# A gated product written without gaps, an fp32 tanh for GpSimd and a later turn for ScalarE's output copies, in an RG-LRU and gated linear unit kernel

## The chip, the cores and the metric

The kernel runs on one core of a Trainium2 chip. Five engines work at the same time, each through its own instructions in order: TensorE (PE in the profile, with its weight loads as PEld), VectorE (DVE), ScalarE (ACT), GpSimd (POOL) and SyncE (SP), which here only issues DMA transfers. The metric is the device time of one execution in microseconds (us); lower is better.

## The reference

Inputs are x, r_gate and i_gate, each 4 x 6336 x 256 in fp32, a vector a_param of 256, and three weights. The first half is a gated linear recurrence over time, the second half a gated linear unit with a causal convolution of 5 taps on its gate.

```python
log_a = 8.0 * sigmoid(r_gate) * log(clip(sigmoid(a_param), 1e-6, 1 - 1e-6))
a_t = exp(log_a)
x_gated = sqrt(maximum(1 - a_t * a_t, 1e-6)) * sigmoid(i_gate) * x
for t in range(S):
    h = a_t[:, t] * h + x_gated[:, t];  y[:, t] = h
gate_pre = sum(conv_w[k] * shifted(y, 4 - k) for k in range(5))
out = (sigmoid(gate_pre) * (y @ w_val)) @ w_out
```

## The kernel before

**Windows.** The 4 x 6336 = 25344 tokens are cut into 50 windows of 512 tokens (the last has 256). In a window, partition p holds the 4 tokens 4p to 4p+3 (index j), so that a load or a store is 4 KB without gaps for each partition.

**The operations of a window**, in the order in which they depend on each other, with their engines and lines:

- `load` (SP, L164): three transfers of 512 KB, r and i into the tile `ri`, x into `xt`, three buffers each.
- `tanh` (ACT, L238): one instruction over both gates, 2048 elements for each partition, fp32 in, bf16 out, into `tri`. Sigmoids are built as (1 + tanh(z/2)) / 2.
- `u2` (POOL): L245 adds 1 to the i half of `tri`, bf16 in, fp32 out, into the single buffer `t1` (named t in the profile); L246 multiplies that by x, bf16 out, into the ring `uring`.
- `srT` (PE, L226): 8 transposes bring the r half to channels on partitions. `exp` (ACT, L261) makes a_t from it, two instructions of 512 elements, into the ring `aring`; it reads the transposed tile with a step, so that tokens come out in their order in time.
- `e` (POOL, L267): a_t squared, fp32, into `ering`. `sq` (ACT, L276 or L282): the square root 0.5 sqrt(1 - e), written as bf16 over `ering`. Sqrt stands in another function table than Tanh and Exp, so each change costs a table load on ACT. The roots of several windows are done together, as a unit.
- `uT` (PE, L226): 8 transposes of `uring`. `scan` (DVE): for each of the two channel halves, L299 multiplies uT (PSUM, read with a step) by the root into `xg`, and L304 scans the recurrence in time, into the ring `yring` in bf16.
- `conv` (PE, L331): 10 matmuls with diagonal weights into `gp`. `tg` (ACT, L338): tanh of the gate. `val` (PE, L347): y times w_val, 4 matmuls into PSUM.
- `gv` (DVE, L356): (tg + 1) times val into `gv`, the left operand of the last product. tg and val have tokens in order of time, t = 4p + j; gv has the layout [j, h, p], so that the 128 tokens with the same j stand side by side.
- `out` (PE, L368): for each half of a window (index q), 4 matmuls with w_out into the PSUM tile `ops`. `osb` copies it to SBUF, on DVE (L379) or on ACT (L381). `store` (SP, L385).

**What sets the order.** `make_plan` (L29 to L116) is a list scheduler that runs when the program is built. It holds a cost for each operation (COST, L20), simulates the five engines, and always takes the candidate with the smallest start time, then the smallest priority number (`min(cands)`, L104). The instructions are then written out in the order of these planned start times, so each engine's queue is fixed. A cost changes no instruction, only the order. The dependencies that the plan sees, with buffer counts, are the lists of pairs: ("u2", -NTRI) means that u2 of three windows before must be done. Both engines are offered for `osb` at L86 and L87, with priority 0.5 for each; on ACT, `tg` has 0, `exp` 1, `tanh` 3 and `sq` -1.

**Units of square roots.** A unit starts when DVE has little left to scan (`low`, L97) and enough windows are ready: at least MIN_UNIT (L19), 1, 2, 3 and 4 for the first four units, 4 for each later one, or when the rings of NS = 11 windows are full (`stuck`).

**Buffers in PSUM.** srT, uT, xg, gp, val and ops have one buffer each, so a writer on PE waits for the reader on DVE or ACT of the window (or the half) before.

Of the kernel before, what the change touches and what calls it, by code (L numbers as in the profile page):

```python
# [8 lines left out]
P = 128  # L9
WIN = 512  # L10
SUB = WIN // P
CONV_K = 5
C_SCALE = 8.0
NS = 11
NY = 7
NIN = 3
NTRI = 3
NOSB = 3
MIN_UNIT = [1, 2, 3, 4]  # L19
COST = dict(load=3.9, tanh=1.9, u2=3.3, srT=0.5, uT=0.5, exp=1.45, e=2.15, scan=3.75, conv=2.45, tg=1.0,  # L20
            val=0.95, gv=1.2, out=0.5, osbD=0.68, osbA=0.6, sq=0.88, sq0=0.2, table=1.3, store=1.3,
            sem=0.15, dma=2.2)
FP32 = mybir.dt.float32
BF16 = mybir.dt.bfloat16
ACT = mybir.ActivationFunctionType
ALU = mybir.AluOpType


def make_plan(frac):  # L29

    nw = len(frac)
    nq = [max(1, round(2 * f)) for f in frac]
    qwin = [(g, i) for g in range(nw) for i in range(nq[g])]
    qlast = [sum(nq[:g + 1]) - 1 for g in range(nw)]
    done, nxt, free = {}, {}, {}
    order, units = [], []
    mode = "E"  # L40

    def at(op):
        return nxt.get(op, 0)

    while True:
        cands = []

        def cand(op, eng, dur, deps, prio, i, n=1):
            t = 0.0
            for d in deps:  # L50
                if d[1] < 0:
                    continue
                if d not in done:
                    return
                t = max(t, done[d] + COST["sem"])
            if eng == "ACT" and op != "osb" and (op == "sq") != (mode == "S"):
                dur = dur + COST["table"]
            cands.append((max(free.get(eng, 0.0), t), prio, op, eng, dur, i, n))

        def per_window(op, eng, prio, deps, limit=nw):  # L60
            g = at(op)
            if g < limit:
                cand(op, eng, COST[op] * frac[g], [(d, g + o) for d, o in deps], prio, g)

        nsq = at("sq")
        per_window("load", "DMA", 0, [("tanh", -NIN), ("u2", -NIN)])
        per_window("tanh", "ACT", 3, [("load", 0), ("srT", -NTRI), ("u2", -NTRI)])
        per_window("u2", "POOL", 1, [("tanh", 0), ("uT", -NS)])
        per_window("srT", "PE", 0, [("tanh", 0), ("exp", -1)])
        per_window("exp", "ACT", 1, [("srT", 0), ("scan", -NS), ("e", -NS)])  # L70
        per_window("e", "POOL", 0, [("exp", 0), ("scan", -NS)])
        per_window("uT", "PE", 1, [("u2", 0), ("scan", -1)], nsq)
        per_window("scan", "DVE", 2, [("uT", 0), ("sq", 0), ("val", -NY), ("conv", 1 - NY)], nsq)
        per_window("conv", "PE", 3, [("scan", 0), ("tg", -1)])
        per_window("tg", "ACT", 0, [("conv", 0), ("gv", -2)])
        per_window("val", "PE", 2, [("conv", 0), ("gv", -1)])
        g = at("gv")
        if g < nw:
            cand("gv", "DVE", COST["gv"] * frac[g],
                 [("tg", g), ("val", g), ("out", qlast[g - 2] if g >= 2 else -1)], 1, g)  # L80
        q = at("out")
        if q < len(qwin):
            cand("out", "PE", COST["out"], [("gv", qwin[q][0]), ("osb", q - 1)], 1, q)
        q = at("osb")
        if q < len(qwin):
            for e, eng in (("D", "DVE"), ("A", "ACT")):  # L86
                cand("osb", eng, COST["osb" + e], [("out", q), ("store", qwin[q][0] - NOSB)], 0.5, q)  # L87
        g = at("store")
        if g < nw:
            cand("store", "DMA", COST["store"] * frac[g], [("osb", qlast[g])], -1, g)  # L90

        n = at("e") - nsq
        if n and mode == "E":
            all_in = at("exp") == nw
            stuck = at("e") == at("exp") and (all_in or ("scan", at("exp") - NS) not in done
                                              and at("exp") >= NS)
            low = (nsq - at("scan")) * (COST["scan"]) <= 2 * COST["table"] + COST["sq"] * n  # L97
            enough = n >= min(MIN_UNIT[min(len(units), len(MIN_UNIT) - 1)], nw - nsq)
            if stuck or (low and enough):
                cand("sq", "ACT", COST["sq0"] + COST["sq"] * sum(frac[nsq:nsq + n]),  # L100
                     [("e", nsq + n - 1)], -1, nsq, n)
        if not cands:
            break
        t, prio, op, eng, dur, i, n = min(cands)  # L104
        free[eng] = t + dur
        order.append((t, op, i, eng, n))
        nxt[op] = i + n
        for k in range(i, i + n):
            done[(op, k)] = t + dur + (COST["dma"] if eng == "DMA" else 0.0)
        if op == "sq":  # L110
            units.append(n)
        if eng == "ACT" and op != "osb":
            mode = "S" if op == "sq" else "E"
    assert at("store") == nw
    order.sort(key=lambda o: o[0])
    return order, qwin  # L116
# [3 lines left out]
def kernel(  # L120
# [11 lines left out]
    nc = tc.nc  # L132
    B, S, D = x.shape
# [10 lines left out]
    ntok = [min(WIN, T - g * WIN) for g in range(nwin)]  # L144

    segs = []
    for g in range(nwin):
        t0, t1 = g * WIN, g * WIN + ntok[g]
# [3 lines left out]
    plan, qwin = make_plan([n / WIN for n in ntok])  # L152

    const = ctx.enter_context(tc.tile_pool(name="const", bufs=1))
    inp = ctx.enter_context(tc.tile_pool(name="inp", bufs=3))
    live = {}
# [10 lines left out]
    with tc.manual_schedule():  # L167
# [19 lines left out]
        with tc.tile_pool(name="ps_setup", bufs=1, space=bass.MemoryType.PSUM) as ps_setup:  # L187
# [6 lines left out]
                                    op0=ALU.mult, op1=ALU.add)  # L194
            nc.vector.tensor_scalar(out=ksig[:], in0=ksig[:], scalar1=1e-6, scalar2=1.0 - 1e-6,
                                    op0=ALU.max, op1=ALU.min)
# [9 lines left out]
        for h in range(H):  # L206
            for kk in range(CONV_K):
                nc.vector.tensor_scalar(out=diag[:, h, kk, :], in0=ident_f[:], scalar1=wcol[:, h, kk:kk + 1],
                                        scalar2=None, op0=ALU.mult)
# [4 lines left out]
        work = ctx.enter_context(tc.tile_pool(name="work", bufs=2))  # L214
# [5 lines left out]
        uring = rings.tile([P, NS, SUB, D], BF16, name="uring")  # L220
        yring = rings.tile([P, H, NY * WIN], BF16, name="yring")

        def transposes(dst, src, g):
            for h in range(H):
                for j in range(ntok[g] // P):
                    nc.tensor.transpose(out=dst[:, h, j * P:(j + 1) * P],  # L226
                                        in_=src[:, j, h * P:(h + 1) * P],
                                        identity=ident_b[:])
# [5 lines left out]
        def op_tanh(g, eng, n):  # L234
            nj = ntok[g] // P
            ri = live.pop(("ri", g))
            tri = inp.tile([P, 2, SUB, D], BF16, name="tri", tag="tri", bufs=NTRI)
            nc.scalar.activation(out=tri[:, :, 0:nj, :], in_=ri[:, :, 0:nj, :], func=ACT.Tanh, scale=0.5)  # L238
            live["tri", g] = tri

        def op_u2(g, eng, n):
            nj = ntok[g] // P
            xt, tri = live.pop(("xt", g)), live["tri", g]
            t1 = work.tile([P, SUB, D], FP32, name="t1", tag="t1", bufs=1)
            nc.gpsimd.tensor_scalar(out=t1[:, 0:nj, :], in0=tri[:, 1, 0:nj, :], scalar1=1.0, scalar2=None, op0=ALU.add)  # L245
            nc.gpsimd.tensor_tensor(out=uring[:, g % NS, 0:nj, :], in0=t1[:, 0:nj, :], in1=xt[:, 0:nj, :],  # L246
                                    op=ALU.mult)

        def op_srT(g, eng, n):
            srT = psum.tile([P, H, WIN], BF16, name="srT", tag="srT", bufs=1)  # L250
            transposes(srT, live["tri", g][:, 0], g)
            live["srT", g] = srT

        def by_token(t, h, g):
# [96 lines left out]
        def op_gv(g, eng, n):  # L351
            gv = work.tile([P, SUB, H, P], BF16, name="gv", tag="gv", bufs=2)
            tg, val = live.pop(("tg", g)), live.pop(("val", g))
            nj = ntok[g] // P
            for hs in ([slice(0, H)] if nj == SUB else [slice(h, h + 1) for h in range(H)]):
                nc.vector.scalar_tensor_tensor(  # L356
                    out=gv[:, 0:nj, hs, :].rearrange("c j h p -> c (h p) j"),
                    in0=tg[:, hs, 0:ntok[g]].rearrange("c h (p j) -> c (h p) j", j=nj), scalar=1.0,
                    in1=val[:, hs, 0:ntok[g]].rearrange("c h (p j) -> c (h p) j", j=nj), op0=ALU.add, op1=ALU.mult)
            live["gv", g] = gv  # L360

        def op_out(q, eng, n):
# [20 lines left out]
        def op_store(g, eng, n):  # L383
            nj = ntok[g] // P
            nc.sync.dma_start(of[g * WIN:g * WIN + nj * P, :].rearrange("(p j) d -> p j d", j=nj),  # L385
                              live.pop(("osb", g))[:, 0:nj, :])

        ops_by_name = dict(load=op_load, tanh=op_tanh, u2=op_u2, srT=op_srT, exp=op_exp, e=op_e, sq=op_sq,
                           uT=op_uT, scan=op_scan, conv=op_conv, tg=op_tg, val=op_val, gv=op_gv,
                           out=op_out, osb=op_osb, store=op_store)  # L390
        for (t, op, i, eng, n) in plan:
# [31 lines left out]
```

## Time and profile before

| | |
|---|---|
| runs | 521.2 and 520.99 us, median 521.1 |
| the profiled execution | 518.84 us, span 517.1 us |
| mean granted TensorE clock | 0.826 |
| instructions | 5526 |
| moved by DMA | 104.44 MB, mean 202 GB/s |

The span runs from the first to the last instruction of one profiled execution. A row of a group names the line, the engine, the operation, out<-in with partitions x elements and type, and the count; behind the first bar come busy time and the mean of one in ns, behind the second the idle time of the engine just before these instructions and what ended it. A row of a stage gives its limits, its length, and for each engine the busy time with the count of instructions; behind them the granted clock (1.00 is full speed), the busy share of the 16 DMA engines, and GB/s. A row of waits reads: who waited <- for whom: total us, times, longest. A row of the timeline has start, duration, engine, line, operation and, in brackets, the idle time before it with what ended it. A row of one line's durations has min/median/max in ns.

### The profile page before, as it was taken

The page shows a single profiled execution, that of the slowest core. Times are in us where ns is not written, and L with a number is a line of the kernel's source. Part 1 is how long each engine was busy: PE and PEld are TensorE (multiplying, and loading weights), DVE is VectorE, ACT ScalarE, POOL GpSimd, SP SyncE. Part 2 cuts the span into 40 slices and gives each one's busy share as a digit, 9 for nine tenths or more (in the row PEclk, how much of TensorE's full clock was granted, in tenths as well). Part 3 has the DMA queues.
Part 4 walks back from the last instruction along what each step waited for, and adds up shares of the span by engine and source line. Part 5 has one row for each costly group of instructions (what it writes and reads, how often), then busy time and mean ns, then how long its engine had stood idle before and what let it go on. Part 6 is the DMA issues. An engine that isn't in the chain of part 4 may idle for free.

```text
span 517.1 us, 5526 instructions
## 1 busy us (share of the span) xinstructions
PE 322.3 (62%) x1971; PEld 181.2 (35%) x1971; DVE 451.9 (87%) x320; ACT 325.3 (63%) x312; POOL 347.8 (67%) x158
## 2 busy tenths in 40 slices
PE   1342865667565576667767665775766766756563
PEld 0222433334333343434433333433433333423232
DVE  3243999978999979999989999999999979999993
ACT  6969667498665774847575685597476594365221
POOL 4999969969965965948773986957948859400000
PEclk9975779876987976989886888798887887899875
DMA  8975754869845467457755774575845651201112
GB/s 281 380 249 207 259 205 148 302 227 326 317 157 215 164 230 259 162 190 252 264 181 210 268 264 170 196 288 189 296 166 200 209 184 75 82 35 47 81 41 103
DMA packets 29386, 104.44 MB, mean 202 GB/s; under 512 B 3239, under 2 KB 3758, under 8 KB 29358
## 3 DMA queue, kind: packets, MB, share of 16 engines
q1 hardware_dynamic: 28814, 103.83, 55.9%
q0 software_dynamic: 544, 0.26, 0.4%
q8 instruction: 15, 0.25, 0.2%
q14 instruction: 13, 0.11, 0.1%
HBM read 78.39 MB, written 25.95 MB: 202 GB/s over the span
## 4 chain that ended last, share of the span: by engine, by line
DVE 45%; issue 31%; PE 12%; ACT 4%; DMA 4%; SPq 0%; DVEq 0%; ACTq 0%
DVE gv L356 19%; DVE yring L304 11%; DVE xg L299 10%; DVE osb L379 4%; PE ops L368 4%; DMA out_dram<-osb 3%; PE gp L331 3%; PE val L347 3%; ACT tri L238 2%; PE uT L226 1%; DMA ri<-in_i_gate_dram 1%; PE srT L226 1%; ACT aring L261 1%; ACT osb L381 0%; ACT ering L282 0%
## 5 line engine op out<-in xcount | busy, mean ns | idle before, releaser
L356 DVE SCALAR_TENSOR_TENSOR gv<-tg,val 128x1024 bf16<-128x1024 bf16 (+1 forms) x51 | 232.9, 4574 | 10.7 <-ACT tg L338 5.1
L267 POOL TENSOR_TENSOR ering<-aring 128x1024 f32<-128x1024 f32 (+1 forms) x50 | 93.8, 1878 | 94.3 <-ACT aring L261 90.0
L245 POOL TENSOR_SCALAR t<-tri 128x1024 f32<-128x1024 bf16 (+1 forms) x50 | 137.2, 2745 | 20.8 <-ACT tri L238 16.2
L331 PE MATMUL gp<-yring,diag 128*128 128x512 bf16 (+13 forms) x580 | 143.8, 402 | 4.3 <-DVE yring L304 4.2
L304 DVE TENSOR_TENSOR_SCAN yring<-aring,yring,xg 128x512 bf16<-128x512 f32 (+4 forms) x98 | 120.6, 1231 | 3.5
L368 PE MATMUL ops<-wo,gv 128*128 128x256 bf16 x396 | 76.1, 327 | 72.3 <-DVE gv L356 37.9
L246 POOL TENSOR_TENSOR uring<-t,xt 128x1024 bf16<-128x1024 f32 (+1 forms) x50 | 116.7, 2334 | 4.2
L381 ACT COPY osb<-ops 128x512 f32<-128x512 f32 x53 | 31.0, 585 | 126.4 <-PE ops L368 104.8
L347 PE MATMUL val<-yring,wv 128*128 128x512 bf16 (+1 forms) x200 | 65.1, 459 | 61.4 <-DVE gv L356 61.4
L238 ACT ACTIVATE tri<-ri 128x2048 bf16<-128x2048 f32 (+1 forms) x50 | 93.9, 1896 | 1.4 <-DMA ri<-in_i_gate_dram 1.4
L299 DVE TENSOR_TENSOR xg<-uT,ering 128x512 f32<-128x512 bf16 (+1 forms) x100 | 76.0, 760 | 20.1 <-ACT ering L282 15.0
L331 PEld LDWEIGHTS <-diag 128*128 128x128 bf16 x580 | 59.2, 112 | 74.4 <-issue 36.3
L338 ACT ACTIVATE tg<-gp 128x1024 bf16<-128x1024 f32 (+1 forms) x50 | 50.8, 1016 | 47.1 <-PE gp L331 46.9
L368 PEld LDWEIGHTS <-gv 128*128 128x128 bf16 x396 | 42.5, 113 | 98.5 <-DVE gv L356 57.5
L261 ACT ACTIVATE aring<-srT,khf 128x512 f32<-128x512 bf16 (+1 forms) x100 | 72.1, 776 | 6.8 <-PE srT L226 5.6
L226 PE MATMUL srT<-ident_b,tri 128*128 128x128 bf16 x396 | 35.5, 241 | 28.5 <-ACT tri L238 28.3
L347 PEld LDWEIGHTS <-wv 128*128 128x128 bf16 x200 | 21.7, 110 | 82.4 <-issue 72.7
L226 PE MATMUL uT<-ident_b,uring 128*128 128x128 bf16 x396 | 36.6, 246 | 21.6 <-DVE xg L299 21.6
L379 DVE COPY osb<-ops 128x512 f32<-128x512 f32 x46 | 35.8, 778 | 15.1 <-PE ops L368 15.1
L282 ACT ACTIVATE ering<-ering,b 128x3072 bf16<-128x3072 f32 (+2 forms) x24 | 47.7, 2031 | 1.1 <-POOL ering L267 1.0
L226 PEld LDWEIGHTS <-tri 128*128 128x128 bf16 x396 | 30.2, 109 | 39.6 <-ACT tri L238 29.7
L226 PEld LDWEIGHTS <-uring 128*128 128x128 bf16 x396 | 30.8, 112 | 33.8 <-issue 21.1
(31 smaller groups left out, 55.8 us busy)
## 6 DMA issues: line engine op xcount, KB each, us to landing
ri<-in_r_gate_dram SPq DMA_DIRECT2D x49, 512.0 KB, 5.0
ri<-in_i_gate_dram SPq DMA_DIRECT2D x49, 512.0 KB, 5.8
xt<-in_x_dram SPq DMA_DIRECT2D x49, 512.0 KB, 5.5
out_dram<-osb SPq DMA_DIRECT2D x49, 512.0 KB, 3.0
ri<-in_r_gate_dram SPq DMA_DIRECT2D x1, 256.0 KB, 3.4
ri<-in_i_gate_dram SPq DMA_DIRECT2D x1, 256.0 KB, 4.2
xt<-in_x_dram SPq DMA_DIRECT2D x1, 256.0 KB, 4.0
out_dram<-osb SPq DMA_DIRECT2D x1, 256.0 KB
```

The source lines that it names most:

```text
L226: nc.tensor.transpose(out=dst[:, h, j * P:(j + 1) * P], in_=src[:, j, h * P:(h + 1) * P], identity=ident_b[:])
L238: nc.scalar.activation(out=tri[:, :, 0:nj, :], in_=ri[:, :, 0:nj, :], func=ACT.Tanh, scale=0.5)
L245: nc.gpsimd.tensor_scalar(out=t1[:, 0:nj, :], in0=tri[:, 1, 0:nj, :], scalar1=1.0, scalar2=None, op0=ALU.add)
L246: nc.gpsimd.tensor_tensor(out=uring[:, g % NS, 0:nj, :], in0=t1[:, 0:nj, :], in1=xt[:, 0:nj, :], op=ALU.mult)
L261: nc.scalar.activation(out=aring[:, g % NS, h, 0:ntok[g]].rearrange("c (p j) -> c p j", j=nj), in_=by_token(srT, h, g), func=ACT.Exp, scal ...
L267: nc.gpsimd.tensor_tensor(out=ering[:, g % NS, :, 0:ntok[g]], in0=a, in1=a, op=ALU.mult)
L299: nc.vector.tensor_tensor(out=xg[:, 0:ntok[g]].rearrange("c (p j) -> c p j", j=nj), in0=by_token(uT, h, g), in1=nring[:, g % NS, h * WIN:h ...
L304: nc.vector.tensor_tensor_scan(out=yring[:, h, y0 + c0:y0 + c1], data0=aring[:, g % NS, h, c0:c1], data1=xg[:, c0:c1], initial=0.0 if fres ...
L331: nc.tensor.matmul(out=gp[:, h, c0:c1], lhsT=diag[:, h, kk, :], rhs=yring[:, h, src:src + c1 - c0], start=(sh == 0), stop=(kk == 0 and k = ...
L347: nc.tensor.matmul(out=val[:, m, 0:ntok[g]], lhsT=wv[:, hk, m * P:(m + 1) * P], rhs=yring[:, hk, y0:y0 + ntok[g]], start=(hk == 0), stop=( ...
L356: nc.vector.scalar_tensor_tensor(out=gv[:, 0:nj, hs, :].rearrange("c j h p -> c (h p) j"), in0=tg[:, hs, 0:ntok[g]].rearrange("c h (p j) - ...
L368: nc.tensor.matmul(out=ops[:, e, :], lhsT=gv[:, 2 * i + e, hk, :], rhs=wo2[:, hk, :], start=(hk == 0), stop=(hk == H - 1))
```

## The change

Four things are changed.

1. `gv`: the same product, with the innermost loop over (h p) in place of j. The output is written without gaps; tg is read with a step of 4 bf16 elements, val with a step of 4 fp32 elements.
2. `tanh` becomes two instructions: the r half into `tr` (bf16, three buffers), the i half into `ti` (fp32, two buffers). `u2` adds 1 in place in `ti`, fp32 to fp32; `t1` goes. The plan's tanh now needs u2 of two windows before.
3. The planner's offer of `osb` on ACT has priority 4 in place of 0.5.
4. MIN_UNIT gets a fifth value, 5, for all later units, and the costs of tanh, e, scan and gv are other numbers.

```diff
-MIN_UNIT = [1, 2, 3, 4]
-COST = dict(load=3.9, tanh=1.9, u2=3.3, srT=0.5, uT=0.5, exp=1.45, e=2.15, scan=3.75, conv=2.45, tg=1.0,
-            val=0.95, gv=1.2, out=0.5, osbD=0.68, osbA=0.6, sq=0.88, sq0=0.2, table=1.3, store=1.3,
+MIN_UNIT = [1, 2, 3, 4, 5]
+COST = dict(load=3.9, tanh=2.1, u2=3.3, srT=0.5, uT=0.5, exp=1.45, e=1.95, scan=3.95, conv=2.45, tg=1.0,
+            val=0.95, gv=1.3, out=0.5, osbD=0.68, osbA=0.6, sq=0.88, sq0=0.2, table=1.3, store=1.3,
...
-        per_window("tanh", "ACT", 3, [("load", 0), ("srT", -NTRI), ("u2", -NTRI)])
+        per_window("tanh", "ACT", 3, [("load", 0), ("srT", -NTRI), ("u2", -2)])
...
-                cand("osb", eng, COST["osb" + e], [("out", q), ("store", qwin[q][0] - NOSB)], 0.5, q)
+                cand("osb", eng, COST["osb" + e], [("out", q), ("store", qwin[q][0] - NOSB)],
+                     0.5 if e == "D" else 4, q)
...
-            tri = inp.tile([P, 2, SUB, D], BF16, name="tri", tag="tri", bufs=NTRI)
-            nc.scalar.activation(out=tri[:, :, 0:nj, :], in_=ri[:, :, 0:nj, :], func=ACT.Tanh, scale=0.5)
-            live["tri", g] = tri
+            tr = inp.tile([P, SUB, D], BF16, name="tr", tag="tr", bufs=NTRI)
+            ti = inp.tile([P, SUB, D], FP32, name="ti", tag="ti", bufs=2)
+            nc.scalar.activation(out=tr[:, 0:nj, :], in_=ri[:, 0, 0:nj, :], func=ACT.Tanh, scale=0.5)
+            nc.scalar.activation(out=ti[:, 0:nj, :], in_=ri[:, 1, 0:nj, :], func=ACT.Tanh, scale=0.5)
+            live["tr", g], live["ti", g] = tr, ti
...
-            xt, tri = live.pop(("xt", g)), live["tri", g]
-            t1 = work.tile([P, SUB, D], FP32, name="t1", tag="t1", bufs=1)
-            nc.gpsimd.tensor_scalar(out=t1[:, 0:nj, :], in0=tri[:, 1, 0:nj, :], scalar1=1.0, scalar2=None, op0=ALU.add)
-            nc.gpsimd.tensor_tensor(out=uring[:, g % NS, 0:nj, :], in0=t1[:, 0:nj, :], in1=xt[:, 0:nj, :],
+            xt, ti = live.pop(("xt", g)), live.pop(("ti", g))
+            nc.gpsimd.tensor_scalar(out=ti[:, 0:nj, :], in0=ti[:, 0:nj, :], scalar1=1.0, scalar2=None, op0=ALU.add)
+            nc.gpsimd.tensor_tensor(out=uring[:, g % NS, 0:nj, :], in0=ti[:, 0:nj, :], in1=xt[:, 0:nj, :],
                                     op=ALU.mult)
...
-            transposes(srT, live["tri", g][:, 0], g)
+            transposes(srT, live.pop(("tr", g)), g)
...
                 nc.vector.scalar_tensor_tensor(
-                    out=gv[:, 0:nj, hs, :].rearrange("c j h p -> c (h p) j"),
-                    in0=tg[:, hs, 0:ntok[g]].rearrange("c h (p j) -> c (h p) j", j=nj), scalar=1.0,
-                    in1=val[:, hs, 0:ntok[g]].rearrange("c h (p j) -> c (h p) j", j=nj), op0=ALU.add, op1=ALU.mult)
+                    out=gv[:, 0:nj, hs, :].rearrange("c j h p -> c j (h p)"),
+                    in0=tg[:, hs, 0:ntok[g]].rearrange("c h (p j) -> c j (h p)", j=nj), scalar=1.0,
+                    in1=val[:, hs, 0:ntok[g]].rearrange("c h (p j) -> c j (h p)", j=nj), op0=ALU.add, op1=ALU.mult)
```

## The prediction

> **What bounds the kernel now.** I read the page's busy shares first, then the idle time of each engine by stage, the groups by shape, and last who waits for whom.
>
> ```profile
> PE 322.3 (62%) x1971; PEld 181.2 (35%) x1971; DVE 451.9 (87%) x320; ACT 325.3 (63%) x312; POOL 347.8 (67%) x158
> ```
>
> VectorE (DVE) is busy 451.9 of 517.1 us, no other engine over 348. The stages show that its 65.2 us of idle time lie mostly at the start:
>
> ```profile
> core 0: us, PE busy (x) PEld busy (x) DVE busy (x) ACT busy (x) POOL busy (x), PEclk, DMA share, GB/s
> 0.00:30.00 30.00, 9.54 (x57) 5.83 (x57) 9.46 (x22) 23.65 (x22) 22.06 (x17) 1.00 0.85 306
> 30.00:60.00 30.00, 13.85 (x88) 8.65 (x88) 15.61 (x11) 21.95 (x20) 29.49 (x13) 0.66 0.67 240
> 60.00:450.00 390.00, 260.72 (x1624) 146.94 (x1625) 369.29 (x253) 255.98 (x243) 295.22 (x129) 0.83 0.61 215
> ```
>
> Up to 60 us DVE works 25.1 us (34.9 idle); after that it is idle 65.2 - 34.9 = 30.3 us of 457.1, 6.6%. So the middle is a queue of DVE work with small gaps. What that work is, by shape:
>
> ```profile
> line engine op names shapes xcount | busy us, mean ns | idle before us <-releasers
> L356 DVE SCALAR_TENSOR_TENSOR gv<-tg,val 128x1024 bf16<-128x1024 bf16 x49 | 230.5, 4704 | 8.7 <-ACT tg L338 5.1 <-PE val L347 3.5
> L304 DVE TENSOR_TENSOR_SCAN yring<-aring,yring,xg 128x512 bf16<-128x512 f32 x90 | 115.2, 1280 | 3.2
> L299 DVE TENSOR_TENSOR xg<-uT,ering 128x512 f32<-128x512 bf16 x98 | 74.9, 764 | 20.1 <-ACT ering L282 15.0 <-PE uT L226 3.3
> L379 DVE COPY osb<-ops 128x512 f32<-128x512 f32 x46 | 35.8, 778 | 15.1 <-PE ops L368 15.1
> ```
>
> Half of DVE's time is one instruction per window, the gated product gv: 4.70 us for 1024 elements a partition, where the product xg takes 0.76 us for 512. The durations by line separate a fixed part from a price per element:
>
> ```profile
> L356 DVE SCALAR_TENSOR_TENSOR gv<-tg,val x51: 1290/4700/4747, 28.4 to 508.7; 128x1024 bf16<-128x1024 bf16 x49, 128x256 bf16<-128x256 bf16 x2
> L299 DVE TENSOR_TENSOR xg<-uT,ering x100: 433/700/997, 19.3 to 499.3; 128x512 f32<-128x512 bf16 x98, 128x256 f32<-128x256 bf16 x2
> ```
>
> gv costs (4.70 - 1.29) us / 768 = 4.44 ns an element, xg (0.700 - 0.433) us / 256 = 1.04 ns with 0.17 us fixed. Both lines reorder tokens, in different ways. xg reads uT out of PSUM with a step of 128 bf16 (256 bytes) and writes without gaps. gv reads both inputs without gaps and writes bf16 with an innermost step of 256 elements (512 bytes). So the slow part of gv is its strided write; a strided PSUM read has no extra cost in these rows.
>
> Who stands behind gv:
>
> ```profile
> ACT osb L381 <- PE ops L368: 104.8, 34, 5.6
> PE val L347 <- DVE gv L356: 61.4, 23, 4.4
> PE ops L368 <- DVE gv L356: 37.9, 13, 5.2
> PE ops L368 <- DVE osb L379: 26.9, 16, 3.6
> ```
>
> TensorE (PE) waits for gv as the reader that frees `val` and as the input of `out`, and ScalarE (ACT) waits behind PE.
>
> **The change part by part.**
>
> *The gated product, turned round.* The same 51 instructions and elements; the write becomes gapless, and the reads step by 4 elements (8 bytes of tg in SBUF, 16 bytes of val in PSUM). No row shows a strided SBUF read by DVE, so its cost is bounded: from below by 0.67 us, the shortest copy of half as many elements out of PSUM (L379, 665 ns minimum, quoted below), from above by today's 4.70. I take the rate of xg, the nearest row, as it too is a two-input DVE product with a strided PSUM input: 0.17 + 1024 x 1.04 ns = 1.23 us. Sum: 49 x 1.23 + 2 x 0.43 = 61.1 in place of 232.9, so DVE falls to 451.9 - 232.9 + 61.1 = 280.1 us. The saved 172 us lie on the path that sets the end, but not all of it can be kept, since ACT and POOL come next.
>
> The Trainium skill, SBUF — State Buffer, section Specifications (TRN2), speaks of 16-byte lines in SBUF that need two hits each for full rate, and of 8-byte lines in PSUM. By it the 512-byte write is slow, as the row of gv shows; tg's 8-byte step still hits each line twice; but val's 16-byte step would touch a new PSUM line at every element. The row of xg, with 256 bytes between elements, shows no such loss on DVE. By the rule gv would keep a large part of its price (the third rival); by the row it would not.
>
> *The tanh in two instructions.*
>
> ```profile
> L238 ACT ACTIVATE tri<-ri x50: 1062/1913/1939, 7.9 to 438.7; 128x2048 bf16<-128x2048 f32 x49, 128x1024 bf16<-128x1024 f32 x1
> L245 POOL TENSOR_SCALAR t<-tri 128x1024 f32<-128x1024 bf16 x49 | 135.8, 2771 | 20.8 <-ACT tri L238 16.2 <-PE gp L331 3.3 <-PE ops L368 0.2
> L246 POOL TENSOR_TENSOR uring<-t,xt 128x1024 bf16<-128x1024 f32 x49 | 115.4, 2356 | 4.1
> L261 ACT ACTIVATE aring<-srT,khf 128x512 f32<-128x512 bf16 x98 | 71.1, 781 | 6.8 <-PE srT L226 5.6 <-issue 1.2
> L267 POOL TENSOR_TENSOR ering<-aring 128x1024 f32<-128x1024 f32 x49 | 92.7, 1895 | 77.3 <-ACT aring L261 73.0 <-DVE xg L299 4.3
> ```
>
> Two of 1.06 us replace one of 1.91: +0.21 us, 50 times, +10.5 us on ACT. The transposes of the r half can begin 0.85 us sooner; the i half is ready 0.2 us later. An fp32 output is not shown for Tanh, but Exp writes fp32 in 0.78 us for 512, so I add nothing (bounds -2 to +5 us in total).
>
> *The +1 on GpSimd (POOL), now fp32 to fp32.* The row for bf16 input is 2.77 us, more than the two-input fp32 product ering with 1.90. With one fp32 input the price lies between half of that, 0.95 us (an estimate: half the data read), and 2.77. I take 1.90: POOL falls by 49 x 0.87 = 43 us to 305; by the low bound to 258; by the high bound it stays at 348. The buffer `t1` goes; `ti` with two buffers lets tanh of window g start only when u2 of g-2 is done. The instructions queued behind that wait on ACT are exp, sq and tg; POOL at 6.2 us a window clears u2 in time as long as it isn't the bound, so I put nothing.
>
> *Output copies and larger units.*
>
> ```profile
> L381 ACT COPY osb<-ops x53: 579/586/593, 34.1 to 512.8; 128x512 f32<-128x512 f32 x53
> L379 DVE COPY osb<-ops x46: 665/692/916, 35.8 to 500.5; 128x512 f32<-128x512 f32 x46
> L282 ACT ACT_TABLE_LOAD x13 | 16.7, 1283 | 0.2
> L338 ACT ACT_TABLE_LOAD x11 | 14.1, 1283 | 1.3 <-DVE gv L356 1.1
> ```
>
> The planner's order on ACT decides ties by priority; 4 in place of 0.5 puts an ACT copy behind tanh (3) too. A copy that ACT gives up costs 0.69 us on DVE in place of 0.585. With square-root units of 1, 2, 3, 4 windows and then 4 each, 50 windows make 14 units, and the page's 13 loads of L282 and one of L276 agree; with 5 each they make 12. Two units fewer save 4 loads of 1.28 us, -5.1 us on ACT. A unit of 5 holds ACT 1 us longer; behind it stand tg and exp, whose readers (gv, e) have other windows to work on, so nothing is added; without that cover it would be about 8 x 1 us. No DMA is added; loads and stores keep their sizes, but their place in SP's queue follows the plan's new times. The transfers need 55.9% of 517.1 = 289 us:
>
> ```profile
> q1 hardware_dynamic: 28814, 103.83, 55.9%
> ```
>
> *The sum.* ACT with all its copies: 325.3 + 10.5 - 5.1 = 330.7. If n copies move to DVE until both are equal: 330.7 - 0.585 n = 280.1 + 0.69 n, n = 40, both 308 us. That is the new bound, with POOL at 305 and DMA at 289 below it. To 308 comes the start, where DVE idles 35 us for upstream work that the change leaves alone, and gaps. After the start the gaps are 6.6% now with one bounding engine; with two equal ones and in-order queues I take one and a half times that, 10% or 31 us, as the long waits for gv go. Span: 308 + 35 + 31 = 374. The profiled execution took 518.84 us, 1.7 over its span, and the median of the runs is 2.3 above that: 374 + 4 = **378 us**. Its own range: below, the start counted by ACT (14.4 us idle up to 60 us) and gaps of 6.6% (20): 308 + 14 + 20 + 4 = 346; above, gaps of 20%: 308 + 35 + 62 + 4 = 409.
>
> **The rivals.**
>
> *POOL becomes the bound.*
>
> ```profile
> 9.95 2.77 POOL L245 TENSOR_SCALAR t<-tri 128x1024 f32<-128x1024 bf16 x1 [6.86 <-ACT tri L238]
> ```
>
> If the add stays at 2.77 us, POOL's 348 us follow 10 us of start. Behind its last square come two table loads (2.6), two windows of xg and scan (2 x 2 x 2.04 = 8.2), conv (2.3), gv (1.2), two copies (1.4) and, as an estimate, 4 for tg, out and the store: 20 us. With gaps of 5% (17): 348 + 10 + 17 + 20 + 4 = 399 us. For it: the 2.77 may come from the operation and not from bf16. Against: the fp32 product with two inputs is faster than this add with one.
>
> *PE at a low clock becomes the bound.* The same ten conv matmuls take 2.33 us or 3.86 us:
>
> ```profile
> 274.38 1.86 PE L347 MATMUL val<-yring,wv 128*128 128x512 bf16 x4 [4.42 <-DVE gv L356]
> 279.47 3.86 PE L331 MATMUL gp<-yring,diag 128*128 128x512 bf16 x10
> 255.03 2.33 PE L331 MATMUL gp<-yring,diag 128*128 128x512 bf16 x10
> 258.27 1.03 PE L347 MATMUL val<-yring,wv 128*128 128x512 bf16 x4
> 283.17 0.61 PE L226 MATMUL srT<-ident_b,tri 128*128 128x128 bf16 x8
> 283.61 0.60 PE L368 MATMUL ops<-wo,gv 128*128 128x256 bf16 x4
> ```
>
> A window at the fast rate needs 2.33 + 2 x 0.61 (srT and uT are alike) + 2 x 0.60 + 1.03 = 5.8 us. Scaled by 3.86/2.33 that is 9.6 us. A granted clock of 0.83 between 1.0 and 0.5 makes a third slow: 7.1 us, 49.5 windows 350 us; with 35 us of start and 7% gaps, 350 + 35 + 25 + 4 = 414 us. Against it: such slow stretches follow waits for gv (274.38 above), which get shorter. The Trainium skill, TensorE: Matmul & The Clock Gate, section Part 1, says likewise that activity releases the throttle; the trace agrees with its ten matmuls at 3.86 us soon after a wait of 4.42 us. By the rule a busier PE would keep the fast rate, 5.8 us x 49.5 = 287 us (an estimate), and be no bound.
>
> *Strided reads keep part of the price.* If the new reads cost half of what the strided write costs now, 2.22 ns an element, gv takes 0.17 + 2.27 = 2.44 us, DVE has 280 + 49 x 1.21 = 339 us beside ACT's 331, and no copy moves: 339 + 35 + 34 + 4 = 412 us. At two thirds, 2.96 ns, gv takes 3.2 us, DVE 377, the time 377 + 35 + 38 + 4 = 454. At the whole price nothing is won: 521. For it stands that no row shows a strided SBUF read by DVE; against it the strided PSUM read of xg. This is the case in which the page on SBUF quoted above would be right on val.
>
> *Slower than before.* Each strided input costs what the strided write costs, one after the other: 2 x 4.44 ns an element, gv 9.1 us, 49 x 4.4 = +216 us on DVE: about 735 us. It is slower from a gv of about 4.9 us on (2% of 521 is 10.4 us, over 49 windows). Against it: xg.
>
> **How the numbers follow.** Forecast 0.66 (346 to 409 us); POOL 0.10 (399); PE 0.12 (414); gv at 2 to 3.5 us 0.07 (412 to 454); gv unchanged 0.03 (521); slower 0.02. The likeliest gives 378. Low 346, high 430: the first four cases lie within it but for gv above about 2.7 us (0.03) and a forecast that proves too cautious (0.05). About 2% can be told from no change here. Faster by over 2%: 0.95; within 2%: 0.03; slower: 0.02.
>
> **What would show it.** Right: gv near 1.2 us in the groups; DVE and ACT both near 310 us busy with about 13 ACT copies left; 12 square-root units; the add on POOL under 2.0 us; waits for gv nearly gone. Wrong: gv over 2 us; POOL busy over 90% of the span (add still 2.77); PE in first place with a clock under 0.8; or DVE and ACT at 310 as said but gaps over 20%, which would be an order of the queues that doesn't fit.

## The result and the profile after

The changed kernel takes 416.73 us (median of 416.49 and 416.96) where the kernel before took 521.1: a ratio of 0.800, with a 95% interval of 0.796 to 0.803. The prediction had 378 us, in a range of 346 to 430. The profiled execution has a span of 415.2 us and took 416.96 us.

The first section of the page after, busy time and share of the span of each engine:

```profile
PE 281.1 (68%) x1938; PEld 166.9 (40%) x1971; DVE 303.2 (73%) x351; ACT 304.3 (73%) x323; POOL 346.5 (83%) x158
```

DVE fell from 451.9 to 303.2 us and ACT stands at 304.3, close to the 308 of the prediction's sum for both. But POOL has 346.5 us, the 347.8 of before, and is now the busiest engine. Where it works, from the stages up to the end of its last instruction and behind it (length, then busy time of each engine with its count):

```profile
core 0: us, PE busy (x) PEld busy (x) DVE busy (x) ACT busy (x) POOL busy (x), PEclk, DMA share, GB/s
0.00:356.00 356.00, 233.46 (x1637) 139.94 (x1666) 256.55 (x300) 284.72 (x296) 346.52 (x158) 0.89 0.78 275
356.00:415.20 59.20, 47.65 (x302) 26.97 (x305) 46.64 (x52) 19.59 (x28) 0.00 (x0) 0.96 0.28 113
```

In its first 356 us POOL is idle for 9.5 us in all, 4.5 of them before the first tanh is ready; so it sets the pace. Then it is done, and the kernel runs on for 59 us without it, with DVE and PE working through windows that are still queued. These two rows are the whole result: a bound of 356 us that POOL's work sets, with the add at its old price, and a rest of 59 us that is something else. The groups by shape that answer to those of before:

```profile
L247 POOL TENSOR_SCALAR ti<-ti 128x1024 f32<-128x1024 f32 x49 | 135.8, 2771 | 4.5 <-ACT ti L241 4.5
L248 POOL TENSOR_TENSOR uring<-ti,xt 128x1024 bf16<-128x1024 f32 x49 | 115.5, 2358 | 4.1
L269 POOL TENSOR_TENSOR ering<-aring 128x1024 f32<-128x1024 f32 x49 | 92.4, 1895 | 0.0
L358 DVE SCALAR_TENSOR_TENSOR gv<-tg,val 128x1024 bf16<-128x1024 bf16 x49 | 59.3, 1209 | 17.1 <-ACT tg L340 16.3 <-PE val L349 0.7
L240 ACT ACTIVATE tr<-ri 128x1024 bf16<-128x1024 f32 x49 | 52.1, 1062 | 1.0 <-DMA ri<-in_r_gate_dram 1.0
L241 ACT ACTIVATE ti<-ri 128x1024 f32<-128x1024 f32 x49 | 51.8, 1058 | 53.0 <-POOL uring L248 52.7 <-DMA ri<-in_i_gate_dram 0.4
L383 ACT COPY osb<-ops 128x512 f32<-128x512 f32 x22 | 12.8, 582 | 19.3 <-issue 11.9 <-PE ops L370 6.6 <-ACT tg L340 0.8
L284 ACT ACT_TABLE_LOAD x11 | 14.1, 1283 | 0.2
```

The gated product takes 1.21 us in place of 4.70. The add on POOL takes 2771 ns with fp32 input, to the nanosecond what it took with bf16. From the list of waits:

```profile
ACT ti L241 <- POOL uring L248: 54.0, 26, 4.3
DVE osb L381 <- PE ops L370: 53.6, 33, 5.6
PE gp L333 <- ACT tg L340: 42.3, 17, 8.3
PE val L349 <- DVE gv L358: 6.6, 12, 0.9
```

The wait of PE for gv has shrunk from 61.4 to 6.6 us. In its place ACT waits 54 us for POOL's product before the tanh of the i half. That is the new two-buffer limit on `ti`: a late POOL holds up ACT's queue, in which tg stands too, and PE waits 42.3 us for tg. By itself the limit is not where the time goes: in the run with the bf16 tanh below, which does not have it, ACT waits 29.0 us for the load of the i gate instead, and the time is no shorter.

How far DVE is behind POOL shows in two answers with the instructions of one line each, up to 300 us and from there: first the product into `uring` on POOL, then gv on DVE.

```profile
0.00:300.00 300.00, 98.99 (x42) 0.87 0.81 285
300.00:415.20 115.20, 17.82 (x8) 0.96 0.45 165
```

```profile
0.00:300.00 300.00, 37.60 (x31) 0.87 0.81 285
300.00:415.20 115.20, 22.39 (x20) 0.96 0.45 165
```

At 300 us POOL has begun 42 windows and gv 31: a backlog of 11 windows.

### The profile page after: what moved, and what is told of

Same layout as the page of the kernel before. It is cut to its first block, busy times and chain, and to the rows that moved or that the text cites. A ratio compares the mean times of both kernels' runs of the same rounds, so it can differ in the third digit from the quotient of the medians.

```text
span 415.2 us, 5490 instructions
## 1 busy us (share of the span) xinstructions
PE 281.1 (68%) x1938; PEld 166.9 (40%) x1971; DVE 303.2 (73%) x351; ACT 304.3 (73%) x323; POOL 346.5 (83%) x158
## 4 chain that ended last, share of the span: by engine, by line
POOL 50%; PE 18%; issue 15%; ACT 10%; DVE 4%; DMA 0%; POOLq 0%; DVEq 0%
POOL ti L247 22%; POOL uring L248 15%; POOL ering L269 13%; PE gp L333 10%; PE val L349 3%; ACT ering L284 3%; PE ops L370 3%; ACT tg L340 2%; DVE osb L381 1%; DVE gv L358 1%; PE srT L227 1%; ACT L340 1%; ACT ti L241 1%; ACT L284 1%; DVE yring L306 1%
## 5 line engine op out<-in xcount | busy, mean ns | idle before, releaser
L333 PE MATMUL gp<-yring,diag 128*128 128x512 bf16 (+8 forms) x564 | 132.7, 382 | 44.2 <-ACT tg L340 42.3
L247 POOL TENSOR_SCALAR ti<-ti 128x1024 f32<-128x1024 f32 (+1 forms) x50 | 137.2, 2745 | 4.5 <-ACT ti L241 4.5
L248 POOL TENSOR_TENSOR uring<-ti,xt 128x1024 bf16<-128x1024 f32 (+1 forms) x50 | 116.8, 2336 | 4.2
L241 ACT ACTIVATE ti<-ri 128x1024 f32<-128x1024 f32 (+1 forms) x50 | 52.5, 1049 | 54.4 <-POOL uring L248 54.0
L381 DVE COPY osb<-ops 128x512 f32<-128x512 f32 x77 | 52.5, 681 | 53.8 <-PE ops L370 53.6
L370 PE MATMUL ops<-wo,gv 128*128 128x256 bf16 x396 | 62.9, 283 | 22.4 <-DVE osb L381 14.0
L358 DVE SCALAR_TENSOR_TENSOR gv<-tg,val 128x1024 bf16<-128x1024 bf16 (+1 forms) x51 | 60.0, 1178 | 17.1 <-ACT tg L340 16.3
L227 PE MATMUL srT<-ident_b,tr 128*128 128x128 bf16 x396 | 34.0, 235 | 31.2 <-ACT aring L263 16.0
L240 ACT ACTIVATE tr<-ri 128x1024 bf16<-128x1024 f32 (+1 forms) x50 | 52.7, 1054 | 1.0 <-DMA ri<-in_r_gate_dram 1.0
L284 ACT ACTIVATE ering<-ering,b 128x3072 bf16<-128x3072 f32 (+2 forms) x22 | 47.3, 2190 | 4.4 <-POOL ering L269 4.3
L227 PEld LDWEIGHTS <-tr 128*128 128x128 bf16 x396 | 29.0, 106 | 43.0 <-issue 19.7
```

Of the source, the lines that this page charges most:

```text
L227: nc.tensor.transpose(out=dst[:, h, j * P:(j + 1) * P], in_=src[:, j, h * P:(h + 1) * P], identity=ident_b[:])
L247: nc.gpsimd.tensor_scalar(out=ti[:, 0:nj, :], in0=ti[:, 0:nj, :], scalar1=1.0, scalar2=None, op0=ALU.add)
L284: nc.scalar.activation(out=nring[:, sl:sl + k, 0:H * WIN], in_=ering[:, sl:sl + k].rearrange("p s h t -> p s (h t)"), func=ACT.Sqrt, scale ...
L333: nc.tensor.matmul(out=gp[:, h, c0:c1], lhsT=diag[:, h, kk, :], rhs=yring[:, h, src:src + c1 - c0], start=(sh == 0), stop=(kk == 0 and k = ...
L358: nc.vector.scalar_tensor_tensor(out=gv[:, 0:nj, hs, :].rearrange("c j h p -> c j (h p)"), in0=tg[:, hs, 0:ntok[g]].rearrange("c h (p j) - ...
L370: nc.tensor.matmul(out=ops[:, e, :], lhsT=gv[:, 2 * i + e, hk, :], rhs=wo2[:, hk, :], start=(hk == 0), stop=(hk == H - 1))
```

## The experiments

The theory after the result has two halves. **A:** gv gave the whole gain, and POOL, whose add is as slow as ever, is the bound. **D:** the 59 us behind POOL are a backlog that the order of the plan builds up. The rivals are named with the runs.

**The gated product alone**, in the kernel before:

```diff
-                    out=gv[:, 0:nj, hs, :].rearrange("c j h p -> c (h p) j"),
+                    out=gv[:, 0:nj, hs, :].rearrange("c j h p -> c j (h p)"),
...
```

> The kernel before with the gated product turned round and nothing else. Theory A (the whole gain comes from gv; then GpSimd is the bound, and its fp32 input, the split tanh, the copy priority and the larger units give nothing or cost time): GpSimd's 348 us nearly without gaps, and since the old plan lets the scan follow u2 by 5 to 7 windows where the new one lets it follow by up to 9, a shorter rest behind GpSimd's last instruction (30 to 40 us where it is 60 us): 390 to 405 us. Rival B (all four parts are needed): over 425 us.

Measured: 397.07 us, a ratio to the kernel before of 0.765 (0.762 to 0.768). One of the four parts gives more than all four together:

```profile
PE 273.6 (69%) x1938; PEld 166.9 (42%) x1971; DVE 283.0 (72%) x320; ACT 322.1 (82%) x312; POOL 347.0 (88%) x158
```

POOL has 347.0 us busy and begins its last product at 356.1 us, in the changed kernel at 354.7; the gain over the changed kernel lies behind that. Theory A holds, and theory B falls.

**All but the gated product**: the changed kernel with the strided write.

```diff
-                    out=gv[:, 0:nj, hs, :].rearrange("c j h p -> c j (h p)"),
+                    out=gv[:, 0:nj, hs, :].rearrange("c j h p -> c (h p) j"),
...
```

> The changed kernel with the strided write of gv put back: split tanh, fp32 add, copy priority and larger units stay. Theory A: VectorE is the bound again with 452 us and some 25 to 30 more copies (17 to 21 us), 520 to 550 us, no faster than before. Rival B: under 505 us.

Measured: 525.47 us, ratio 1.012 (1.008 to 1.015), within A's 520 to 550. The other three parts without the first make the kernel 1% slower: DVE, still the bound, has 31 copies more. Groups of this run:

```profile
L358 DVE SCALAR_TENSOR_TENSOR gv<-tg,val 128x1024 bf16<-128x1024 bf16 x49 | 230.6, 4706 | 6.0 <-PE val L349 6.0
L381 DVE COPY osb<-ops 128x512 f32<-128x512 f32 x77 | 59.4, 771 | 19.8 <-PE ops L370 19.8
```

**The tanh in bf16 again**, in the changed kernel, in the same plan (the buffers go back with it, `tri` with three and `t1` with one):

```diff
...
-            nc.scalar.activation(out=tr[:, 0:nj, :], in_=ri[:, 0, 0:nj, :], func=ACT.Tanh, scale=0.5)
-            nc.scalar.activation(out=ti[:, 0:nj, :], in_=ri[:, 1, 0:nj, :], func=ACT.Tanh, scale=0.5)
...
+            nc.scalar.activation(out=tri[:, :, 0:nj, :], in_=ri[:, :, 0:nj, :], func=ACT.Tanh, scale=0.5)
...
+            nc.gpsimd.tensor_scalar(out=t1[:, 0:nj, :], in0=tri[:, 1, 0:nj, :], scalar1=1.0, scalar2=None, op0=ALU.add)
```

> The changed kernel with one tanh instruction for both gates in bf16 and the add reading bf16, in the plan of the changed kernel. Theory A (the add costs GpSimd 2.77 us whatever the input type): GpSimd busy 347 us again, time 410 to 418 us, ScalarE 10 us less busy. Rival C (fp32 is worth something elsewhere, in the transposes that can start earlier or in the buffers): over 425 us.

Measured: 421.12 us, ratio to the kernel before 0.811 (0.809 to 0.814), so about 1% slower than the changed kernel: between the two theories, and outside the 410 to 418 that A gave. POOL's busy time is 346.7 us as A said; ACT lost only 4.6 us of the 10: its instructions overlap in the trace where they follow each other without a wait, so a pair of tanhs lasts 2.01 us from begin to end, about 0.1 more than the single one, and not 2.12. Over half of the difference in time sits at the start. The first add of each kernel, here and then in the changed kernel:

```profile
9.74 2.77 POOL L246 TENSOR_SCALAR t<-tri 128x1024 f32<-128x1024 bf16 x1 [6.64 <-ACT tri L239]
```

```profile
7.59 2.77 POOL L247 TENSOR_SCALAR ti<-ti 128x1024 f32<-128x1024 f32 x1 [4.50 <-ACT ti L241]
```

With one instruction, the first tanh waits until both gates have landed; in two, the r half runs while the i gate is still on its way. POOL starts 2.15 us later and ends at 359.3 instead of 355.9. That is 3.4 of the 4.0 us between the spans (419.2 and 415.2). So the split is worth about 1%, more than half of it through the earlier start, and the add gains nothing from its input's type. Where the other 1.2 us of POOL's delay come from stays open.

**The true cost of u2 in the plan**, in the changed kernel:

```diff
-COST = dict(load=3.9, tanh=2.1, u2=3.3, ...
+COST = dict(load=3.9, tanh=2.1, u2=5.15, ...
```

> The changed kernel with one number of the plan set to what the trace shows: u2 costs 5.15 in place of 3.3; no instruction differs, only the order. Theory D (the 60 us behind GpSimd's last instruction are a backlog of some 9 windows that the plan builds up because it takes GpSimd for faster than it is; with the true cost the plan's scan follows u2 by 5 to 6 windows): GpSimd still busy 347 us, the rest behind it 30 to 40 us, 390 to 400 us. Rival E (the backlog comes from waits on the chip and not from the order): 412 to 420 us as before this edit.

Measured: 393.72 us, ratio 0.759 (0.756 to 0.761): 23 us less than the changed kernel, by the order alone. POOL is busy 346.5 us as before and ends at 356.8; the rest behind it is 36.0 us in place of 59.2. At 300 us u2 has begun 41 windows and gv 35:

```profile
0.00:300.00 300.00, 96.59 (x41) 0.91 0.82 291
300.00:392.80 92.80, 20.18 (x9) 0.94 0.52 186
```

```profile
0.00:300.00 300.00, 42.45 (x35) 0.91 0.82 291
300.00:392.80 92.80, 17.67 (x16) 0.94 0.52 186
```

Theory D holds, and rival E falls.

**The priority of ScalarE's copies, undone:**

```diff
-                     0.5 if e == "D" else 4, q)
+                     0.5, q)
```

> The changed kernel with priority 0.5 for the copies on ScalarE too, as before the change; nothing else differs. In its plan the scan follows u2 by 6 to 8 windows near the end, instead of 9, and 51 copies in place of 22 are on ScalarE. Theory D: the rest behind GpSimd's last instruction shrinks with that backlog to 40 to 48 us: 397 to 407 us. Rival G (the later turn of the copies is a gain in itself and something else made the backlog): 417 us or more.

Measured: 404.95 us, ratio 0.780 (0.776 to 0.783). The backlog at 300 us is 7 windows (42 and 35), the rest behind POOL 44 us. The later turn of the copies costs 12 us here; rival G falls.

**The larger units, undone:**

```diff
-MIN_UNIT = [1, 2, 3, 4, 5]
+MIN_UNIT = [1, 2, 3, 4]
```

> The changed kernel with MIN_UNIT ending at 4 as before the change; nothing else differs. In its plan the scan follows u2 by 8 windows near the end instead of 9. Theory D: the rest behind GpSimd shrinks by about one window of 5 to 6 us: 408 to 413 us. Rival H (the larger units made the backlog): under 405 us.

Measured: 416.56 us, ratio 0.802 (0.799 to 0.805), no difference. Both expectations miss: the backlog at 300 us went from 11 windows only to 10 (42 and 32), and the rest behind POOL from 59.2 to 58.5 us.

**Both undone:** the two diffs above together.

> The changed kernel with both edits of the order undone, priority 0.5 for the copies on ScalarE and MIN_UNIT ending at 4; gv, the split tanh and the new costs stay. In its plan the scan follows u2 by 5 to 6 windows near the end. Theory D (the time behind GpSimd's last instruction is that backlog, and the two edits made it together): 393 to 401 us, as with gv alone (397). Rival I (the split tanh costs time by itself): over 405 us, near the run with the priority alone undone (405).

Measured: 399.99 us, ratio 0.770 (0.767 to 0.772); backlog 6 windows. It is within 3 us of gv alone, so the two edits of the order explain nearly all of what the changed kernel loses against gv alone, and rival I falls. Undoing the units alone does nothing, but with the priority undone too it is worth another 5 us.

**The add as a sum of two tensors**, with a tile of ones, in the order of the changed kernel:

```diff
+        ones = const.tile([P, SUB, D], FP32, name="ones")
+        nc.vector.memset(ones[:], 1.0)
...
-            nc.gpsimd.tensor_scalar(out=ti[:, 0:nj, :], in0=ti[:, 0:nj, :], scalar1=1.0, scalar2=None, op0=ALU.add)
+            nc.gpsimd.tensor_tensor(out=ti[:, 0:nj, :], in0=ti[:, 0:nj, :], in1=ones[:, 0:nj, :], op=ALU.add)
```

> The changed kernel with GpSimd's add of the constant 1 written as an addition of two tensors, ti plus a tile of fp32 ones, in the same order. Theory A2 (the add's 2.77 us belong to the operation with a scalar operand, not to the data; two tensors in fp32 cost 1.90 us like the square): GpSimd 2.77 to 1.90 us in that line, 305 us busy, its last instruction near 318 us instead of 356, time 370 to 385 us. Rival F (2.77 us is the price of this line's data or place, for instance of writing over its input): 412 to 420 us as before this edit.

Measured: 398.0 us, ratio 0.766 (0.763 to 0.769). Same data and same place, another operation, and 0.41 us less:

```profile
L249 POOL TENSOR_TENSOR ti<-ti,ones 128x1024 f32<-128x1024 f32 x49 | 115.6, 2360 | 4.8 <-ACT ti L243 4.8
L250 POOL TENSOR_TENSOR uring<-ti,xt 128x1024 bf16<-128x1024 f32 x49 | 115.5, 2357 | 3.8
L271 POOL TENSOR_TENSOR ering<-aring 128x1024 f32<-128x1024 f32 x49 | 92.4, 1894 | 0.0
```

Rival F falls. The size was off, and the time lies above the 370 to 385 us expected: two different tensors cost 2.36 us, in fp32 or with a bf16 result; the square, which reads one tensor as both inputs, costs 1.89. So A2's 1.90 came from a row that was not alike, and POOL has 325.6 us, not 305. Of its 21 us less, 19 reach the time; the rest behind POOL is still 61.2 us.

**The same with u2 = 4.25 in the plan**, and with 4.75, which is nearer the measured 4.72 us:

```diff
-COST = dict(load=3.9, tanh=2.1, u2=3.3, ...
+COST = dict(load=3.9, tanh=2.1, u2=4.25, ...
```

> The same with the plan's cost of u2 set to 4.25 (1.90 + 2.36 us), so that the scan follows u2 by 5 to 7 windows in the plan instead of up to 9. Theories A2 and D together: GpSimd 305 us busy, a rest of 35 to 45 us behind it, 358 to 375 us, faster than the form without the new cost. Rival: with GpSimd at 305 us, VectorE and ScalarE at 304 set the time and the order no longer matters: the same time as without the new cost, within 3 us.

> The changed kernel with the two-tensor add and with the measured sum of GpSimd's two instructions in the plan, u2 = 4.75 (2.36 + 2.36 us, where the run before had 4.25). GpSimd 326 us busy and ending near 336 us, the scan 5 to 6 windows behind: 372 to 382 us, 0 to 8 us under the run with 4.25 (381). Rival: the chip's end is set by ScalarE and VectorE and not by the backlog: 381 us or more.

Measured: 381.36 us, ratio 0.733 (0.730 to 0.737), and 377.16 us, ratio 0.725 (0.723 to 0.727). The first is slower than the 358 to 375 expected, because POOL did not fall to 305 us; the second is as expected. Against the order of the changed kernel (398.0) the plan's number alone gives 17 and 21 us. The second of them is the fastest kernel here, 39.6 us under the changed kernel. Its stage behind POOL:

```profile
336.20:374.30 38.10, 27.85 (x193) 16.53 (x191) 31.43 (x37) 14.54 (x20) 0.04 (x1) 0.95 0.29 118
```

**The add on VectorE**, for all windows and for every second one, as an operation of its own in the plan, which here counts 2.36 us for the product, 2.77 for the add on POOL and 0.7 on DVE:

```diff
...
-        per_window("u2", "POOL", 1, [("tanh", 0), ("uT", -NS)])
+        onD = lambda w: True
+        g = at("ad")
+        if g < nw:
+            cand("ad", "DVE" if onD(g) else "POOL", COST["adD" if onD(g) else "ad"] * frac[g], [("tanh", g)], 1, g)
+        per_window("u2", "POOL", 1, [("ad", 0), ("uT", -NS)])
...
+            e.tensor_scalar(out=ti[:, 0:nj, :], in0=ti[:, 0:nj, :], scalar1=1.0, scalar2=None, op0=ALU.add)
...
-            nc.gpsimd.tensor_scalar(out=ti[:, 0:nj, :], in0=ti[:, 0:nj, :], scalar1=1.0, scalar2=None, op0=ALU.add)
...
```

In the second run `onD` is true for every second window.

> The changed kernel with the add of 1 moved from GpSimd to VectorE for all windows, as an operation of its own in the plan (0.7 us), and u2 there at 2.36 us. GpSimd falls to 211 us busy, VectorE rises by 50 times 0.6 to 1.2 us to 333 to 363 us. Theory A (GpSimd alone stood between the prediction's sum and the chip): VectorE and ScalarE set the time, 370 to 395 us. Rival J (the two engines hold each other up when both work in SBUF): the add takes over 1.5 us or GpSimd's products over 2.6 us on average, and the time is over 400 us.

> The same with the add on VectorE for every second window only: GpSimd 279 us busy, VectorE about 320, ScalarE 305. Theory A: all engines are near 300 to 320 us, with 20 us of start and 35 us behind the last square: 365 to 380 us. Rival J: over 390 us.

Measured: 391.61 us, ratio 0.752 (0.747 to 0.756), and 379.16 us, ratio 0.730 (0.727 to 0.732). Both lie in A's ranges. With POOL at 215.3 us DVE is the bound with 350.0; with half the adds there, DVE has 327.1 us, ACT 309.1 and POOL 283.5, and the time is about that of the best kernel. Some holding up between the two engines is to be seen, though less than rival J needed. Durations of the add on DVE and of the product on POOL in the first of the two (min/median/max in ns):

```profile
L252 DVE TENSOR_SCALAR ti<-ti x50: 667/793/2506, 12.0 to 323.5; 128x1024 f32<-128x1024 f32 x49, 128x512 f32<-128x512 f32 x1
```

```profile
L257 POOL TENSOR_TENSOR uring<-ti,xt x50: 1267/2359/2813, 12.8 to 326.2; 128x1024 bf16<-128x1024 f32 x49, 128x512 bf16<-128x512 f32 x1
```

The trace of this run shows where the long ones come from. Three rows from it, an add with no product running on POOL, a product, and an add that begins inside that product:

```profile
273.67 0.67 DVE L252 TENSOR_SCALAR ti<-ti 128x1024 f32<-128x1024 f32 x1
274.47 2.37 POOL L257 TENSOR_TENSOR uring<-ti,xt 128x1024 bf16<-128x1024 f32 x1 [2.06 <-DVE ti L252]
275.98 1.40 DVE L252 TENSOR_SCALAR ti<-ti 128x1024 f32<-128x1024 f32 x1
```

The second add ends 0.54 us after the product. So it is with all 25 of the 49 adds of full size that begin more than 0.05 us before the end of a running product: they end 0.55 us behind it and take 857 to 2506 ns. The other 24 take 667 to 693 ns. The two engines do hold each other up, as rival J says, but on average the add takes 1149 ns and the product 2396, below J's 1.5 and 2.6 us. With every second add on POOL the picture is less clean: three adds on DVE there took 682 to 737 ns inside a running add of POOL.

## Why the prediction was right or wrong

**The range.** The 416.73 us lie within the stated 346 to 430, but not by the path that was forecast. That path ended at 409 us, with DVE and ACT as the bound; they did come to 303 and 304 us, near its 308, but the 356 us of POOL and the 59 us behind it make up the time. The range holds it because it left room for rivals. For the one that came true, POOL as the bound, the sum was 399 us, and no sum had the 59 us; so that the time lies in the range is in part luck.

**What held.** DVE was the bound before, gv's write was the reason, and the new strided reads cost what the sum took for them: 1.23 us was the value taken, 1.21 was measured. The line's busy time fell from 232.9 to 60.0 us, where the sum had 61.1. Its 8-byte step in SBUF and its 16-byte step in PSUM cost nothing beyond xg's 1.04 ns an element. So the rule of SBUF — State Buffer, Specifications (TRN2), in the Trainium skill agrees with these traces for the 512-byte write (4.44 ns an element) and for tg's 8-byte step. Carried over to PSUM's 8-byte lines, as in the prediction's third rival, it does not hold for DVE's reads: there the measured 1.04 ns decide. The tanh pair takes 2.12 us by its two rows, as said, but as the two overlap, ACT paid 4.6 us for it in all and not 10.5. The granted clock rose from 0.826 to 0.899 with a PE busy for 68% of the span in place of 62%, so the rival of a slow PE did not come true; that agrees with the Trainium skill, TensorE: Matmul & The Clock Gate, Part 1, by which activity releases the throttle.

**The step that failed** is the add on POOL: "I take 1.90: POOL falls by 49 x 0.87 = 43 us to 305; by the low bound to 258; by the high bound it stays at 348." The high bound was true, 2771 ns with either type. The nearest row was taken to be the square, which is a different operation and reads a single tensor; the row of the same operation, 2.77 us, was put down to its bf16 input without a row that showed an influence of the type. With that the rival to which the prediction gave 0.10, POOL as the bound, is what happened.

**The second miss** is in that rival's own sum, 399 us. Its start of 10 us was 7.6, its gaps of 17 us about 2, but the rest behind POOL, put at 20 us for a lag of two windows, was 59.2 us. The lag was 11 windows. The prediction gave the plan's new numbers no price beyond four table loads saved, dearer copies on DVE and a general 10% of gaps; it did not ask how many windows the new order lets POOL run ahead. In the kernels above, backlog at 300 us and rest behind POOL's last instruction go together: 11 windows and 59 us (changed kernel), 11 and 61 (sum of two tensors), 10 and 60 (tanh in bf16), 10 and 58 (units undone), 7 and 44 (priority undone), 7 and 43 (sum of two tensors, 4.25 in the plan), 6 and 36 (true cost), 6 and 38 (the best). With gv alone and with both edits undone POOL waits for ACT before its last squares; counted from its last product, it is 5 and 37, 6 and 36. From 11 windows to 6, between the changed kernel and the one with the true cost, the rest falls by 23.2 us, 4.6 us a window. DVE, busy 46.64 of those 59.2 us, is what works the backlog off: between 373.8 and 394.1 us it does so without a gap, in 5.09 us a window.

**Why the plan ran ahead.** It counted u2 as 3.3 us where the chip takes 5.13 (2.77 + 2.36). Setting that one number to 5.15 took the backlog from 11 to 6 windows and 23 us off the time; undoing the later turn of the copies took it from 11 to 7. The wrong number does this only together with the edits of the order: with gv alone and with both edits undone the plan counts 3.3 us too, and the backlog is 5 and 6 windows. Why the copies' turn adds to the backlog in the plan, no run shows by itself.

**Counts.** 22 copies stayed on ACT where 13 were said, and there were 11 table loads in line L284 where 12 units were said; neither changes the sum by more than some 6 us.

## What to carry to other kernels

When the busiest engine is relieved, the time goes to the next one's busy time plus the backlog that is left behind it, so the next engine's costliest instruction deserves a run or a like row before any sum of averages. A price should be taken from a row of the same operation first, and from one of like data only when the operation is known not to matter. In a kernel with a fixed order, a wrong cost in the planner is a cost on the chip: here one corrected number was worth 23 us, and two edits that looked like fine tuning took back 17 us of the 122 that the gated product alone had won.

## What the runs showed of the hardware that was not expected

- GpSimd, 1024 elements a partition: adding a constant takes 2.77 us with bf16 or fp32 input; adding or multiplying two different tensors 2.36 us, with fp32 or bf16 result; a tensor times itself 1.89 us. Here one input and a constant is slower than two inputs.
- VectorE writes bf16 with a step of 512 bytes at 4.44 ns an element, and reads with steps of 8 bytes in SBUF, 16 and 256 bytes in PSUM at 1.04 ns an element, the same in gv and in xg.
- The same add of 1024 fp32 elements in SBUF takes VectorE 667 to 693 ns where no GpSimd product is running; where it begins inside one, it ends 0.55 us behind that product and takes up to 2506 ns (25 of 49, with all adds on VectorE). GpSimd's product beside it goes up to 2813 ns from its 2.36 us. With every second add on VectorE the add's mean there was 1249 ns.
- Two tanhs of ScalarE in a row, 1.06 us each, last 2.01 us from begin to end.
